# Block sums of the keys by one-column matmuls, transposes in two halves of 64 rows, and gate masks of 0 and 1

## The chip, the cores and the metric

The kernel runs on one core of a Trainium2 chip. The core has a matrix engine (TensorE, PE in the profile, with its weight loads listed apart as PEld), a vector engine (VectorE, DVE), an activation engine (ScalarE, ACT), a general engine (GpSimd, POOL), a sync engine that issues transfers (SyncE, SP), and 16 DMA engines. Tiles lie in SBUF; matmuls write to PSUM, which DVE and ACT read and POOL does not. Each engine works through its own list of instructions in order and waits on semaphores for the others. The metric is the device time of one execution in microseconds (us).

## The reference

Two layers follow each other. The first is block-sparse attention over 4 batches, 8 heads, 768 positions of width 64. Each query scores the means of the 12 key blocks of 64, keeps the three best blocks among its own and the earlier ones, adds its own block, and attends causally inside them. The second takes the real part of a two-dimensional Fourier transform of the attention's output, adds it to that output, normalises each row and runs a two-layer ReLU network of width 2048, with a residual.

```python
k_rep = k.reshape(B, H, n_blocks, block, D).mean(axis=3)
gate_scores = np.einsum('bhsd,bhnd->bhsn', q, k_rep)
gate_scores = np.where(causal, gate_scores, -1000000000.0)
top_idx = np.argsort(gate_scores, axis=-1)[..., -top_k:]
...
scores = np.where(mask, scale * np.matmul(q, k.transpose(0, 1, 3, 2)), -1000000000.0)
attn = np.exp(scores - np.max(scores, axis=-1, keepdims=True))
x = np.matmul(attn / (np.sum(attn, axis=-1, keepdims=True) + 1e-09), v)
...
u = x + np.real(np.fft.fft(np.fft.fft(x, axis=1), axis=2))
un = (u - mu) / np.sqrt(var + 1e-06)
return u + np.maximum(un @ w_ch1, 0.0) @ w_ch2
```

## The kernel before

The heads are taken in pairs: 16 pairs P of two heads e, four pairs to a batch b, pairs 0 to 3 being batch 0. A long string, `ORDER`, lists every step by hand as `name:arguments`, and the program walks it once and issues what each step holds; each engine's own order is what `ORDER` leaves of it. So where a step stands in `ORDER` decides what stands behind it on its engine.

The steps of one pair:

- `Lk`, `Lq`, `Lv`: SP issues the loads of keys, queries and values, three tiles deep for keys and queries, two for values.
- `tk`, `tq` (`a_tp`, L292): PE transposes the 128x128 fp32 pieces of keys and queries, six of each, into a PSUM tile `tp` of two banks. There are four such PSUM tiles for everything.
- `ks` (`a_sums`, L297): DVE sums the transposed keys over each block of 64, from PSUM, into `kr12`. `kh` (`a_half`) multiplies these 12 sums by a 0/1 tile and so lays them out by head.
- `kc` (L308, L311) copies the keys to fp16 on ACT, `qc` (L316) the queries to fp32 on DVE, `qs` on POOL to fp16.
- `g` (L335 for pairs 0 to 6, L342 later): the gate scores, fp32 matmuls on PE with 32 output rows each, one to each quarter of the array's columns. `gt` transposes them on DVE into `gt` and clears the blocks that lie in a query's future (a `min` with `lim` for pairs 0 to 6, three fills later). `gx` takes the eight largest of each row, `gl` compares with the third largest (`gl:P,0`) and multiplies with `oth` or `oth2`, which holds -60000 and, at the own block, 0 (`gl:P,1`); `gm` transposes back to `mt`.
- `s` (L409 and L421 for pairs 0 to 6; L414 later): scores. In pairs 0 to 6 the two heads' matmuls each use 64 rows of the array, upper half and lower half, into two banks; the mask is added by further 64-row matmuls of `mt` against `indz`. From pair 7 on the mask rows ride as rows 64 to 95 (`K`, on POOL) and each matmul has 96 rows.
- `e` (L431): the exponential on ACT. `d` (L437): the causal diagonal on POOL. `v` (L449): attention times values on PE. `x`: the division on DVE.

The steps of one batch: `fs`, `fd`, `f` fold the rows and columns on DVE; `y` (L519, L525) and `m` (L552, L553) are the two Fourier matmuls; `u` (L566) adds, `xu` (L578) scales to fp16 on ACT; then the rows are transposed, for batch 0 by PE (`xt`, `t_mm`, L585) with a DVE copy out (`un`, `t_copy`, L590), for the others by DMA. `w` (L629, L631) and `c` (L656) are the two network layers, 16 and 6 large steps per batch, `r` the ReLU, `o` the residual.

`w` of batch 0 is the first work that PE can do without waiting for each pair's chain; in `ORDER` of before it first stands behind the exponentials of pairs 0 to 5.

Of the kernel before, what the change touches and what calls it, by code (L numbers as in the profile page):

```python
# [15 lines left out]
NEG = -60000.0  # L16
# [12 lines left out]
def _consts_np():  # L29
# [22 lines left out]
    oth = np.where(np.arange(9)[:, None] + 3 != nn, NEG, 0.0)[None].repeat(128, 0)  # L52

    lim = np.where(nn[None, 4:8] > np.arange(3, 7)[:, None], -3e38, 3e38)
    lim = lim.reshape(1, 16).repeat(128, 0).astype(np.float32)

    indc = np.zeros((4, 32, 2, NB), np.float32)
    for g in range(4):
        for n in range(NB):
            indc[g, n, g % 2, n] = 1.0  # L60

    own = 2 * np.arange(5)[None, :] + 2 + (p // 64)[:, None]
    oth2 = np.zeros((128, 5, 2, 16), np.float32)
    oth2[:, :, :, 0:NB] = np.where(own[:, :, None, None] != nn, NEG, 0.0)
    ind = np.zeros((2, 32, S), np.float32)
    for e in range(2):
        ind[e, 16 * e:16 * e + NB] = nn[:, None] == (s[None, :] // 64)
    return dict(FS=fs.astype(np.float16), FD=fd.astype(np.float16),
                oth=oth.reshape(128, 108).astype(np.float16),
                lim=lim,  # L70
                indc=indc.reshape(128, 24).astype(np.float16),
                oth2=oth2.reshape(128, 160).astype(np.float16),
# [40 lines left out]
Lk:1 Lq:1 Lk:2 Lq:2 tk:0 ks:0 tq:0 Lq:3 Lk:3 kh:0 qc:0 iz:1 tk:1 qs:0 kc:0 g:0 ks:1 iz:0 gt:0 tq:1  # L113
kc:1 gx:0 Lq:4 Lv:0 Lk:4 Lv:1 kh:1 gl:0,0 tk:2 gl:0,1 gm:0 kc:2 qc:1 s:0,3 s:0,2 ks:2 e:0,3 qs:1
tq:2 Lq:5 Lk:5 s:0,5 qc:2 g:1 e:0,5 e:0,2 kh:2 s:0,4 gt:1 qs:2 s:0,0 e:0,4 gx:1 s:0,1 d:0,2 tq:3
gl:1,0 e:0,0 gl:1,1 tk:3 gm:1 e:0,1 d:0,0 qc:3 g:2 d:0,3 kc:3 d:0,5 s:1,5 gt:2 d:0,4 s:1,0 e:1,5
qs:3 ks:3 s:1,4 e:1,0 tq:4 d:0,1 gx:2 vc:0 e:1,4 s:1,3 qc:4 s:1,1 Lv:2 e:1,3 s:1,2 gl:2,0 kh:3
tk:4 gl:2,1 e:1,2 d:1,3 gm:2 g:3 d:1,4 ks:4 d:1,0 v:0 d:1,5 gt:3 vc:1 kc:4 gx:3 e:1,1 s:2,5 Lv:3
Lq:6 LF:0 Lq:7 Lk:6 Lk:7 LT:0 s:2,3 kh:4 gl:3,0 e:2,5 gl:3,1 s:2,4 e:2,3 d:1,1 x:0 tq:5 qs:4 e:2,4
g:4 d:2,3 gm:3 qc:5 s:2,0 d:2,4 s:2,2 d:1,2 e:2,0 gt:4 d:2,5 tk:5 vc:2 gx:4 e:2,2 s:2,1 ks:5 d:2,0  # L120
Lv:4 Lq:8 Lk:8 s:3,1 e:2,1 v:1 gl:4,0 kh:5 gl:4,1 kc:5 d:2,1 gm:4 d:2,2 s:3,2 x:1 e:3,1 vc:3 g:5
e:3,2 Lv:5 Lc:0 d:3,1 s:3,5 gt:5 s:3,0 fs:0,1 e:3,5 s:3,3 d:3,2 gx:5 e:3,0 s:3,4 fs:1,1 tq:6
gl:5,0 e:3,3 fs:0,0 v:2 gl:5,1 fs:1,0 e:3,4 d:3,3 qc:6 d:3,0 s:4,5 x:2 d:3,4 s:4,4 e:4,5 d:3,5
s:4,0 qs:5 v:3 e:4,0 gm:5 fs:2,0 fs:2,1 e:4,4 s:5,5 x:3 s:4,1 e:5,5 s:5,1 e:4,1 fd:2,0 s:4,2 s:5,0
fs:3,1 e:5,1 fs:3,0 s:5,2 fd:2,1 e:5,0 fd:3,1 s:4,3 fd:3,0 e:5,2 tk:6 f:0,1 f:0,2 e:4,3 Lk:9 Lq:9
tk:7 f:0,3 e:4,2 f:0,0 y:0,1 ks:7 pg:0 W:0 kc:6 y:0,0 tr:0,1 d:4,0 kc:7 d:4,4 d:4,5 ks:6 d:5,5
d:4,1 ty:0,1 tr:0,0 s:5,3 d:5,2 s:5,4 d:4,3 kh:6 W:1 ty:0,0 m:0,2 qs:6 e:5,3 u:0,2 m:0,1 vc:4
e:5,4 m:0,0 u:0,1 xu:0,2 d:5,4 tk:8 d:5,1 d:4,2 u:0,0 xu:0,1 d:5,0 xt:0,2 W:2 g:6 un:0,2 xu:0,0
xt:0,1 gt:6 tq:8 un:0,1 kc:8 xt:0,0 qc:8 tq:7 un:0,0 qs:8 v:4 Lq:10 Lk:10 Lv:6 Lq:11 qc:7 bn:0,3
w:0,4 d:5,3 qs:7 bn:0,1 w:0,5 r:0,4 gx:6 ks:8 w:0,6 r:0,5 gl:6,0 kh:7 gl:6,1 x:4 w:0,7 r:0,6 gm:6  # L130
w:0,3 r:0,7 s:6,5 r:0,3 s:6,1 e:6,5 s:6,3 e:6,1 kh:8 s:6,2 fs:4,0 bn:0,4 w:0,2 e:6,2 d:6,1 X:0
e:6,3 g:7 w:0,0 d:6,5 gt:7 r:0,2 d:6,3 vc:6 gx:7 s:6,4 r:0,0 vc:5 s:6,0 e:6,4 tk:9 Li:0 gl:7,0
Lv:7 tq:9 gl:7,1 e:6,0 gm:7 w:0,11 Lq:12 Lv:8 K:7 qc:9 kc:9 g:8 r:0,11 v:5 gt:8 d:6,0 ks:9 w:0,8
qs:9 gx:8 w:0,10 x:5 r:0,8 d:6,4 d:6,2 gl:8,0 s:7,5 s:7,2 r:0,10 kh:9 fs:4,1 w:0,1 bn:0,5 e:7,5
vc:7 e:7,2 tq:10 gl:8,1 Lv:9 r:0,1 X:1 gm:8 s:7,4 qc:10 w:0,15 d:7,2 e:7,4 K:8 bn:0,0 g:9 r:0,15
s:7,0 w:0,9 gt:9 e:7,0 gx:9 vc:8 tq:11 r:0,9 d:7,0 Lv:10 s:7,1 qc:11 d:7,5 tk:10 d:7,4 e:7,1
gl:9,0 s:7,3 ks:10 v:6 e:7,3 kh:10 gl:9,1 kc:10 gm:9 d:7,3 s:8,4 bn:0,2 d:7,1 w:0,12 vc:9 x:6
e:8,4 K:9 Lv:11 Lk:11 Lq:13 Lq:14 Lk:12 Lk:13 v:7 r:0,12 g:10 x:7 s:8,3 w:0,13 e:8,3 gt:10 nv:0
s:9,4 r:0,13 fs:5,1 s:9,1 fs:7,0 vc:11 w:0,14 e:9,4 fs:6,1 e:9,1 fs:7,1 s:8,1 fs:6,0 fs:5,0
c:0,2,0 r:0,14 fd:7,1 fd:6,1 e:8,1 gx:10 s:9,0 fd:7,0 s:9,2 e:9,0 fd:6,0 s:8,2 gl:10,0 c:0,3,0  # L140
f:1,3 e:9,2 f:1,2 e:8,2 gl:10,1 f:1,0 s:8,0 gm:10 s:9,3 d:8,2 e:8,0 y:1,1 d:8,1 d:9,0 e:9,3 nr:0
c:0,0,0 tr:1,1 ty:1,1 s:9,5 c:0,2,1 e:9,5 d:8,0 d:9,3 tk:11 K:10 s:8,5 c:0,1,0 Lk:14 ks:11 kc:11
# [32 lines left out]
r:3,8 w:3,13 r:3,1 r:3,4 w:3,6 w:3,10 w:3,9 r:3,10 r:3,13 w:3,5 r:3,6 w:3,14 r:3,5 w:3,12 c:3,2,0  # L175
r:3,12 r:3,9 r:3,14 c:3,0,0 w:3,15 c:3,4,0 r:3,15 c:3,1,0 c:3,0,1 c:3,1,1 c:3,5,0 o:3,0 od:3,0
o:3,1 c:3,3,0 od:3,1 o:3,5 od:3,5 c:3,4,1 c:3,2,1 o:3,4 od:3,4 c:3,3,1 c:3,5,1 o:3,3 od:3,3 o:3,2
od:3,2 o:3,6 od:3,6
"""
assert PT_W == 5376 and len(COL) == 42  # L180

# [606 lines left out]
```

## Time and profile before

| | |
|---|---|
| median of two timed runs | 297.85 us (297.19 and 298.51) |
| the profiled execution | 297.41 us, of which the span of its instructions 295.6 us |
| granted TensorE clock in the profile | 1.000 |

The span and the time differ by 1.8 us, which lie around the instructions. Read first the busy shares over the span in 40 slices (a slice is 7.4 us, a digit is tenths of it, 9 is 90% or more):

```profile
## 2 busy tenths in 40 slices
PE   8899999999999999999999999999999999999995
PEld 4566767765676556656757667446666554555453
DVE  2999999986988638987796577714493282700132
ACT  3698989749578841677788843165524250155000
POOL 2267528528776289064753363220303000110000
PEclk9999999999999999999999999999999999999999
DMA  8999999997999727477000005311000052300023
```

A busy PE is not PE at its peak, since matmuls overlap: a matmul of 512 columns takes 379 ns from start to end, but the next one may start after 216 ns. The costliest groups (line, engine, operation, tiles, shape, count, then busy us and mean ns of one, then the idle time before them):

```profile
L629 PE MATMUL h<-unT,w 128*128 128x512 f16 x256 | 85.1, 379 | 0.0
L656 PE MATMUL c<-w_sb,hT 128*128 128x512 f16 x368 | 83.8, 379 | 0.0
L431 ACT ACTIVATE pt<-sc 128x1024 f16<-128x1024 f32 (+1 forms) x96 | 83.3, 923 | 26.6 <-PE sc L414 19.7
```

### The profile page before, as it was taken

What the parts mean: (1) busy time and instruction counts of PE and PEld (TensorE: products, weight loads), DVE (VectorE), ACT (ScalarE), POOL (GpSimd) and SP (SyncE); (2) the same over time, 40 slices, a digit from 0 to 9 for tenths busy, and PEclk for the clock granted to TensorE, in tenths of its full rate; (3) what the DMA queues carried; (4) which work ended last, traced back from release to release, by engine and by line L of the source; (5) the groups of instructions that cost most, each with busy time, mean ns of one, the idle gap of its engine ahead of it and who ended that gap; (6) DMA issues with size and microseconds to landing.
All of it is one profiled execution on the core that took longest, in us unless ns stands there. A gap on an engine that the chain in (4) does not pass through costs nothing.

```text
span 295.6 us, 6738 instructions
## 1 busy us (share of the span) xinstructions
PE 286.5 (97%) x2633; PEld 180.2 (61%) x2633; DVE 192.5 (65%) x597; ACT 164.2 (56%) x205; POOL 111.1 (38%) x286
## 2 busy tenths in 40 slices
PE   8899999999999999999999999999999999999995
PEld 4566767765676556656757667446666554555453
DVE  2999999986988638987796577714493282700132
ACT  3698989749578841677788843165524250155000
POOL 2267528528776289064753363220303000110000
PEclk9999999999999999999999999999999999999999
DMA  8999999997999727477000005311000052300023
GB/s 197 268 228 230 262 245 199 195 230 118 226 185 211 168 55 186 118 164 176 3 0 2 0 9 136 38 72 71 2 1 2 32 103 44 142 0 2 0 91 125
DMA packets 93200, 33.53 MB, mean 113 GB/s; under 512 B 85936, under 2 KB 89968, under 8 KB 93168
## 3 DMA queue, kind: packets, MB, share of 16 engines
q1 hardware_dynamic: 87504, 28.47, 40.6%
q0 software_dynamic: 3664, 4.19, 9.1%
q10 hardware_dynamic: 2000, 0.44, 0.7%
q8 instruction: 21, 0.34, 0.5%
q14 instruction: 11, 0.09, 0.1%
HBM read 28.63 MB, written 6.29 MB: 118 GB/s over the span
## 4 chain that ended last, share of the span: by engine, by line
PE 84%; DVE 7%; ACT 6%; DMA 1%; issue 1%; DVEq 0%; ACTq 0%
PE c L656 26%; PE h L629 19%; PE h L631 10%; PE sc L414 7%; PE av L449 6%; ACT pt L431 5%; PE tp L292 5%; PE yp L519 2%; PE mx L552 2%; DVE q L316 2%; PE mx L553 1%; PE warmps L693 1%; DVE u L566 1%; PE g L342 1%; PE c L648 1%; PE sc L409 1%
## 5 line engine op out<-in xcount | busy, mean ns | idle before, releaser
L431 ACT ACTIVATE pt<-sc 128x1024 f16<-128x1024 f32 (+1 forms) x96 | 83.3, 923 | 26.6 <-PE sc L414 19.7
L629 PE MATMUL h<-unT,w 128*128 128x512 f16 x256 | 85.1, 379 | 0.0
L656 PE MATMUL c<-w_sb,hT 128*128 128x512 f16 x368 | 83.8, 379 | 0.0
L631 PE MATMUL h<-unT,w 128*128 128x256 f16 x256 | 69.7, 272 | 0.4 <-DMA unT<-x 0.4
L641 ACT ACTIVATE hT<-h 128x768 f16<-128x768 f32 x48 | 37.8, 813 | 43.7 <-PE h L631 43.7
L656 PEld LDWEIGHTS <-hT 128*128 128x128 f16 x368 | 35.6, 98 | 39.3 <-issue 0.5
L437 POOL TENSOR_SCALAR_AFFINE_SELECT pt<-pt 128x256 f16<-128x256 f16 x96 | 37.5, 414 | 58.5 <-ACT pt L431 57.6
L629 PEld LDWEIGHTS <-w 128*128 128x128 f16 x256 | 25.0, 97 | 29.2 <-issue 1.3
L668 DVE SCALAR_TENSOR_TENSOR u<-c,rs,u 128x512 f32<-128x512 f32 (+1 forms) x25 | 17.5, 725 | 31.2 <-PE c L656 30.4
L639 DVE TENSOR_SCALAR hT<-h 128x768 f16<-128x768 f32 x16 | 15.3, 955 | 29.7 <-PE h L631 29.6
L578 ACT ACTIVATE x<-u,nm 128x512 f16<-128x512 f32 x24 | 15.9, 715 | 22.5 <-DVE nm L572 22.3
L292 PE MATMUL tp<-id,nat 128*128 128x128 f32 x192 | 27.5, 284 | 0.6 <-ACT pt L431 0.3
L631 PEld LDWEIGHTS <-w 128*128 128x128 f16 x256 | 25.0, 98 | 4.3
L225 POOL TENSOR_SCALAR_AFFINE_SELECT qk<-mt 32x160 f16<-32x160 f16 x72 | 23.1, 341 | 10.8 <-DVE mt L386 9.1
L414 PE MATMUL sc<-qk 96*128 96x512 f16 (+3 forms) x144 | 26.8, 305 | 0.0
L225 POOL TENSOR_SCALAR_AFFINE_SELECT qk<-q 64x768 f16<-64x768 f32 (+1 forms) x25 | 20.6, 825 | 14.8 <-DVE q L316 14.1
L292 PEld LDWEIGHTS tp<-id,nat 128*128 128x128 f32 x192 | 22.2, 146 | 5.7 <-issue 1.6
L449 PE MATMUL av<-v,pt 128*128 128x65 f16 x672 | 23.0, 193 | 0.1
L449 PEld LDWEIGHTS <-pt 128*128 128x128 f16 x672 | 22.0, 97 | 1.7 <-POOL pt L437 0.5
L297 DVE TENSOR_REDUCE kr<-tp 128x12 f32<-128x768 f32 x16 | 15.1, 945 | 5.9 <-PE tp L292 5.9
L222 POOL TENSOR_TENSOR t<-vr,rs 128x6 f32<-128x6 f32 x12 | 2.4, 199 | 43.5 <-DVE rs L609 42.9
L414 PEld LDWEIGHTS <-qk 96*128 96x128 f16 x144 | 13.3, 97 | 8.9 <-issue 0.5
(95 smaller groups left out, 351.2 us busy)
## 6 DMA issues: line engine op xcount, KB each, us to landing
nat<-in_v_dram SPq DMA_DIRECT2D x16, 384.0 KB, 4.7
nat<-in_k_dram SPq DMA_DIRECT2D x31, 192.0 KB, 3.5
nat<-in_q_dram SPq DMA_DIRECT2D x31, 192.0 KB, 3.9
out_dram<-u SPq DMA_DIRECT2D x23, 256.0 KB, 2.1
w_sb<-in_moe_w_ch_dram POOLq DMA_DIRECT2D x2, 1024.0 KB, 10.2
w<-in_moe_w_ch_dram POOLq DMA_DIRECT2D x2, 768.0 KB, 8.4
fs_sb<-c_FS SPq DMA_DIRECT2D x1, 582.0 KB, 5.1
w<-in_moe_w_ch_dram POOLq DMA_DIRECT2D x1, 512.0 KB, 7.3
```

What stands on the lines that cost most here:

```text
L225: nc.gpsimd.affine_select(out=out, in_=in_, pattern=[[0, i] for i in n], base=0, channel_multiplier=0, compare_op=ALU.is_ge, fill=0.0)
L292: nc.tensor.transpose(ps[:, 128 * st:128 * st + 128], src[:, st, :], id32)
L414: nc.tensor.matmul(ps[:, e, co:co + q1 - q0], qk[0:96, e, 1, 128 * jt:128 * jt + 128], qk[0:96, e, 0, q0:q1], start=True, stop=True)
L431: nc.scalar.activation(out=d["pt"][:, o:o + 2 * n].rearrange("p (e c) -> p e c", e=2), in_=d["sc", i][:, :, 0:n], func=AF.Exp, scale=0.125)
L437: nc.gpsimd.affine_select(out=dg, in_=dg, pattern=[[0, 2], [1, 128]], base=0, channel_multiplier=-1, compare_op=ALU.is_ge, fill=0.0)
L449: nc.tensor.matmul(av[:, e, 66 * st:66 * st + 65], pt[:, co:co + 128], vv[:, e, jt, 0:65], start=(cnt == 0), stop=(cnt == 20))
L578: nc.scalar.activation(out=x_b[:, 2 * kp + k2, :], in_=u_b[:, k2, :], func=AF.Identity, scale=0.0625, bias=nm[:, k2:k2 + 1])
L629: nc.tensor.matmul(hp[:, 0:512], w1s, unT[:, dt, 0:512], start=(dt == 0), stop=(dt == NDT - 1))
L631: nc.tensor.matmul(hp[:, 512:768], w1s, unT[:, dt, 512:768], start=(dt == 0), stop=(dt == NDT - 1))
L641: nc.scalar.activation(out=hT, in_=hp, func=AF.Relu)
L656: nc.tensor.matmul(c_ps[b, g[0]][:, st - g[0], :], h_t[b, it][:, 128 * st:128 * (st + 1)], w2_sb[:, it, :], start=(it == 0), stop=(it == N ...
L668: nc.vector.scalar_tensor_tensor(out=o, in0=ps, scalar=st_t[b][1][:, st:st + 1], in1=o, op0=ALU.mult, op1=ALU.add)
```

## The change

1. `a_tp`: each 128x128 transpose becomes two of 64 rows, the upper into one bank of the PSUM tile and the lower into the other; everything that reads the tile does so through `tp_view`. For the keys of pairs 0 to 8 each of them is followed by matmuls of the same 64 rows against a column of ones: 12 fp32 matmuls of one output column per pair.
2. `a_sums` is left out for pairs 0 to 8; `a_half` reads the sums from PSUM.
3. The masks `lt` are 0 or 1; the -60000 has moved into the constants `indc` and `ind`. The own block is filled with 3e38 in `gt` after the maxima are taken and before the comparison, so the multiplication is gone, and with it `oth`, `oth2` and their loads. `lim` gives way to a strided fill.
4. `t_mm` is cut into 64-row transposes in the same way, and `t_copy` for batch 0 becomes two copies of half the size.
5. `ORDER` is rewritten down to the middle of the work on batch 1's second layer; its last 202 steps are the same. In the new one five of pair 6's six score tiles, the gate of pair 7 and `v:5` stand ahead of the first `w`, where before only pairs 0 to 5 and the steps up to `v:4` did; the first row statistics (`bn:0,3`) and the third load of `w_ch1`, which stood ahead of it, now stand behind.

```diff
-            indc[g, n, g % 2, n] = 1.0
+            indc[g, n, g % 2, n] = NEG
...
-        ind[e, 16 * e:16 * e + NB] = nn[:, None] == (s[None, :] // 64)
+        ind[e, 16 * e:16 * e + NB] = np.where(nn[:, None] == s[None, :] // 64, NEG, 0.0)
...
 def a_tp(P, who):
-    d["tp", who] = ps = pst([128, S], f"tp{who}_{P}")
+    d["tp", who] = ps = pst([128, 2, 512], f"tp{who}_{P}")
     for st in range(NST):
-        nc.tensor.transpose(ps[:, 128 * st:128 * st + 128], src[:, st, :], id32)
+        for h in range(2):
+            rows = slice(64 * h, 64 * h + 64)
+            nc.tensor.transpose(ps[:, h, 64 * st:64 * st + 64], src[rows, st, :], id32[rows, rows])
+        for h in range(2 if who == 1 and P < NSUM else 0):
+            rows = slice(64 * h, 64 * h + 64)
+            o = 64 * NST + st
+            nc.tensor.matmul(ps[:, h, o:o + 1], src[rows, st, :], ones[rows, :], start=True, stop=True)
+
+def tp_view(ps):
+    return ps[:, :, 0:64 * NST].rearrange("p h (st c) -> p st h c", c=64)
...
 def a_half(P):
+    if P < NSUM:
+        sums = pairs[P]["tp", 1][:, :, 64 * NST:64 * NST + NST].rearrange("p h (o st) -> p o st h", o=1)
+        tt((kr_s if P < NX else kr2_s)[P % NSLOT][:, :, 0:NB].rearrange("p e (st h) -> p e st h", h=2),
+           sums.to_broadcast([128, 2, NST, 2]), half.rearrange("p e (st h) -> p e st h", h=2), ALU.mult)
+        return
...
 def g_turn(P):
     if P < NX:
-        x = gt.rearrange("p (b n) -> p b n", n=32)[:, 0:4, 4:8]
-        tt(x, x, lim, ALU.min)
+        nc.vector.memset(gt[:, 4:136].rearrange("p (b c) -> p b c", c=33)[:, :, 0:4], -3e38)
...
 def g_less(P, j):
     if j == 0:
-        tt(l, gt, mx[:, :, 2:3].to_broadcast([128, 9 if P < NX else 10, NB]), ALU.is_lt)
-    else:
-        tt(l, l, o, ALU.mult)
+        if P < NX:
+            nc.vector.memset(gt[:, 3:300].rearrange("p (b c) -> p b c", c=33)[:, :, 0:1], 3e38)
+        else:
+            for h in range(2):
+                nc.vector.memset(gt[64 * h:64 * h + 64, 2 + h:172 + h]
+                                 .rearrange("p (b c) -> p b c", c=34)[:, :, 0:17:16], 3e38)
+        return
+    tt(l[:, :, 0:NB], gt[:, 0:nj * w].rearrange("p (j n) -> p j n", n=w)[:, :, 0:NB],
+       mx[:, :, 2:3].to_broadcast([128, nj, NB]), ALU.is_lt)
...
 def t_mm(b, kp):
-    for k2 in range(2):
-        for dt in range(NDT):
-            nc.tensor.transpose(ps[:, dt, 128 * k2:128 * k2 + 128],
-                                x_t[b][:, 2 * kp + k2, 128 * dt:128 * dt + 128], id16)
+    for dt in range(NDT):
+        for k2 in range(2):
+            for h in range(2):
+                rows = slice(64 * h, 64 * h + 64)
+                nc.tensor.transpose(ps[:, h, dt, 64 * k2:64 * k2 + 64],
+                                    x_t[b][rows, 2 * kp + k2, 128 * dt:128 * dt + 128],
+                                    id16[rows, rows])
 def t_copy(b, kp):
-        nc.vector.tensor_copy(out=un_t[b][:, :, 256 * kp:256 * kp + 256], in_=t_ps[b, kp])
+        dst = un_t[b][:, :, 256 * kp:256 * kp + 256].rearrange("p t (k h c) -> p t k h c", h=2, c=64)
+        for h in range(2):
+            nc.vector.tensor_copy(out=dst[:, :, :, h, :], in_=t_ps[b, kp][:, h, 0:NDT, :]
+                                  .rearrange("p t (k c) -> p t k c", c=64))
...
-    nc.scalar.dma_start(lim, dr["lim"].ap().rearrange("p (b n) -> p b n", n=4))
-    nc.scalar.dma_start(oth, dr["oth"].ap().rearrange("p (b n) -> p b n", n=NB))
...
-    nc.sync.dma_start(oth2, dr["oth2"].ap().rearrange("p (b e n) -> p b e n", e=2, n=16))
```

## The prediction

> **What bounds the kernel now.** I read the page first, then a table of stages for the part in which the other engines are full, then the groups of PE, then its order of time. The first line of the page says that PE is busy for 97% of the span:
>
> ```profile
> PE 286.5 (97%) x2633; PEld 180.2 (61%) x2633; DVE 192.5 (65%) x597; ACT 164.2 (56%) x205; POOL 111.1 (38%) x286
> ```
>
> In the order of time the first `w` starts at 58.6. The table of stages up to there (stage, its length, busy time of PE, PEld, DVE, ACT, POOL, the clock, the DMA share) shows another picture:
>
> ```profile
> 12.60:24.00 11.40, 10.92 (x154) 7.20 (x151) 10.96 (x38) 9.93 (x13) 7.19 (x15) 1.00 1.04 235
> 24.00:35.00 11.00, 10.48 (x199) 7.13 (x196) 10.35 (x50) 10.35 (x13) 7.12 (x14) 1.00 1.05 244
> 35.00:45.00 10.00, 9.24 (x182) 7.54 (x182) 9.26 (x25) 9.25 (x13) 2.32 (x5) 1.00 1.03 245
> 45.00:55.00 10.00, 9.16 (x102) 7.06 (x101) 9.62 (x24) 9.83 (x13) 8.25 (x17) 1.00 1.11 205
> ```
>
> DVE, ACT and the DMA engines are all nearly full. PE's busy time holds the latency of each matmul, so I count its own work by the spacing of matmuls: 512, 256 and 128 columns of fp16 take 379, 272 and 219 ns, so a column costs 0.42 ns, and the rest is latency that overlaps. For each kind of step ahead of the first `w` this gives, in us: `tk` 5.9, `tq` 5.9 (nine each, 0.66 a step), `g` 3.4, `s` 12.5 (the two heads side by side), `v` 6.2, `y` 2.5, `m` 2.6, `xt` 1.3, changes of array shape 3.2 (34, priced below): 43.5. With 3.9 of warm-up matmuls PE is idle for 11.2 of 58.6. The same count for all that follows gives 231.4 in the 237.0 that are left; 3.4 of the 5.6 over lie behind the last matmul. So the kernel is an early stage that ACT and DVE set, then PE without a gap.
>
> **What a 64-row step costs.** The rows that price it (the first four are groups: busy us and mean ns of one; the others stand in order of time: start and length of a run of equal instructions):
>
> ```profile
> L292 PE MATMUL tp<-id,nat 128*128 128x128 f32 x192 | 27.5, 284 | 0.6 <-ACT pt L431 0.3
> L292 PEld LDWEIGHTS tp<-id,nat 128*128 128x128 f32 x192 | 22.2, 146 | 5.7 <-issue 1.6 <-ACT pt L431 0.9 <-DVE q L316 0.6
> L335 PEld LDWEIGHTS g<-q,kr 128*32 128x32 f32 x56 | 1.1, 107 | 1.7 <-issue 1.1 <-DVE x L222 0.3 <-ACT pt L431 0.2
> L297 DVE TENSOR_REDUCE kr<-tp 128x12 f32<-128x768 f32 x16 | 15.1, 945 | 5.9 <-PE tp L292 5.9
> ...
> 13.94 0.20 PE L421 MATMUL sc<-mt,indz 64*128 64x32 f16 x4
> ...
> 14.70 0.10 PEld L409 LDWEIGHTS <-qk 64*128 64x128 f16 x2 [0.47 <-issue]
> 14.70 0.39 PE L409 MATMUL sc<-qk 64*128 64x512 f16 x2
> ...
> 64.99 0.27 PE L631 MATMUL h<-unT,w 128*128 128x256 f16 x1
> 65.20 0.23 PE L409 MATMUL sc<-qk 64*128 64x128 f16 x2
> ...
> 67.85 0.27 PE L631 MATMUL h<-unT,w 128*128 128x256 f16 x1
> 68.05 0.48 PE L342 MATMUL g<-q,krb 128*32 128x160 f32 x8
> ```
>
> At 14.70 two matmuls of 512 columns, of 0.38 each, end within 0.39, and two weight loads of 0.09 within 0.10: the upper and the lower 64 rows work at the same time, in both. At 65.20 and 68.05 a matmul starts 0.21 and 0.20 after one of 256 columns that occupies 0.11: a change of array shape costs 0.095, and PE does nothing in it.
>
> An fp32 transpose of 128 columns takes the next one 0.11 later, twice a column of fp16, so 64 columns take 0.055. Its weight load of 128 columns lasts 146 ns where 32 columns last 107: 0.4 ns a column, so 0.05 for the load itself. I take 0.057 for a half, whichever ends last. If halves overlap, six pairs of halves are 0.34 where six transposes are 0.66: 0.31 less. If they don't, 0.68. No row shows an fp32 pair of halves; the nearest are these fp16 pairs in the same two halves, and I take the overlap.
>
> A one-column sum has one column to stream, but its weights are the full 128. `g` has 56 records for 28 matmuls: fp32 goes in two passes, each with its load. So each of the six positions of `tk` takes three loads, 0.171 if halves overlap: 1.03, which is 0.37 more than now; 2.05 if they don't.
>
> The Trainium skill speaks against this in "TensorE: Matmul & The Clock Gate", section "LDWEIGHTS (loading the stationary operand)": a load takes the number of columns over 1.2, whatever the rows, so 107 ns for 128. The rows above contradict it, with 39 ns for 96 more columns. By the page a `tq` would stay at 0.64, `tk` would be 1.92, and the sum below 15 us worse. Its "TensorEngine Tiling (Array Packing)", section "Key Properties", says that changing the tiling mode drains the array; here that is the 0.095.
>
> **The sum on PE.** Ahead of the first `w`: `tk` 9.2, `tq` 3.1, `xt` 0.7 by the new price. The new order also brings forward one `g`, five `s` tiles and `v:5`: 0.3 + 1.7 + 1.2 = 3.2. Shape changes are 32, 3.0. That makes 46.4 against 43.5. Behind it: 3.2 less for what was brought forward; seven `tk` and seven `tq` at 0.31 less, 4.4; 38 shape changes for 22, because transposes now stand as islands of 64 rows among 128-row matmuls, +1.5. So 225.3 against 231.4, 6.1 less. The whole of PE's work falls by 3.2, from 275.0 to 271.8; the other 2.9 is idle time filled early.
>
> **When the first `w` starts.** DVE loses ahead of it eight sums of 0.945 (7.6), six multiplications by `oth` of 0.215 (1.3) and seven `lim` steps of 0.309, for fills like those of L356 to L358 at 0.065 each (about 0.9 for fourteen, so 1.3 net): 10.2. `a_half` now reads PSUM: 0.22 to 0.37 for 24 elements, taken as 0.30, nothing to count. The two half copies of `un` lie between 0.74 and 1.2 for 0.68, three times, at the end of the chain: +0.2 to +1.5, taken as 0.5. So DVE is no longer full. ACT is: between the first exponential and the last `xu` its list grows by one `kc` (two casts of 0.79) and two exponentials (1.03 and 0.39), 3.0 by durations and 2.7 as they overlap. Its idle time in the table is 1.5 + 0.7 + 0.8 + 0.2 = 3.2, of which the first 1.5 lies where `kc` waits for the DVE sum ("ACT qk L308 <- DVE kr L297" in the waits); that wait goes, and what is late next is ACT itself. So the last `xu`, which ends at 55.9, ends at 55.9 + 2.7 - 1.5 = 57.1, or between 55.4 and 58.6. Behind it stand the copy (0.7 and the 0.5) and on PE `s:6,3`, `s:6,2` and `v:5`, 2 us, largely beside it. I take the first `w` where it was, at 58.6, give or take 2.
>
> The removed loads of `lim`, `oth` and `oth2` (8, 27 and 40 KB) cost their issue on queues of ACT and SP; no wait in the profile ends on them, and the load that SP issues behind the last one, the keys of pair 9, is used 25 us after its issue. I count nothing; without that cover it would be 1.1, the time of the issue of `oth2`. The first `tk` runs at half the pace (0.21 from one transpose to the next at 5 us, later 0.11): it would take 2.0 for 1.3, and the first `kh` no longer waits for a sum of 0.9, so these cancel.
>
> Span: 295.6 - 6.1 = 289.5. With the 1.8 around it 291.3, against 297.41 of the same execution; the median stands 0.4 higher. I predict 291.5.
>
> **The rivals.**
>
> *ACT or the loads hold the first `w` back.* For: DMA is full to the first `w`, and the new list has more values (`Lv:6` and on) ahead of it. Up to `Lv:5` and with the first part of `w_ch1` it must move nine keys and queries of 0.39 MB each, six values of 0.39, 1.2 of constants and 1.05 of weights: 11.7 MB, at 228 GB/s 51 us; the second part and `Lv:6` make 13.7 and 60. Against: from pair 5 on, keys and queries had landed 3 us and more ahead of their use. Price: the first `w` at 62, 3.4 later: 295. Chance 0.17.
>
> *DVE and ACT both gain,* with the 3.2 of ACT's idle time gone and the list behind `w` better fed: `w` at 55.5, 288.5. Chance 0.14.
>
> *The fp32 halves don't overlap,* in loads or in matmuls: slower. Then `tk` is 2.05 nine times (+12.5), the other 23 steps gain nothing (+0.6), shape changes +1.3: 289 of PE work for 275. Ahead of `w` 58.6 of work; the early idle time can swallow some 7 of the 15 extra, so `w` starts near 66.5; 230 behind it and the 5.6: 302, so 304 as a time. The point from which it decides: with 7 us of idle time over the 54 positions of nine `tk`, PE sets the early stage once a position costs over 0.30. Chance 0.15.
>
> The change doesn't do what it says if the narrower transposes lose to shape changes: 14 steps at 0.31 against 0.19 each when they stand alone. This is in the forecast, and leaves 0.12 a step; its worst is 1.5 us of the 6.1.
>
> **How the numbers follow.** Forecast 0.54 (288.5 to 294.5); the rivals 0.17, 0.14 and 0.15. The range goes from 286.5 to 298: it leaves out most of the last rival and a twentieth below. About 2% can be told from no change, 291.9: the forecast lies on both sides of it, 0.29 and 0.25; with the better case faster is 0.43, with the late `w` and part of the last rival the same is 0.43, slower 0.14.
>
> **What would show it.** After: runs of six `tk` matmul pairs near 0.35 us and of `tk` with sums near 1.0; no 945 ns sum for pairs 0 to 8; the first `w` near 58.6 with pair 6's exponentials done; ACT over 95% from 13 to 57; PE without gaps behind. The prediction is wrong if weight loads of the two halves come 0.05 apart instead of together, if PE waits for a `nat` load, or if `w` starts past 61.

## The result, and the profile after

| | before | after |
|---|---|---|
| median of two timed runs | 297.85 us | 321.80 us (321.27 and 322.33) |
| profiled execution, its span | 297.41, 295.6 us | 321.27, 319.6 us |
| first exponential | 12.6 us | 17.8 us |
| first `y` | 45.0 us | 64.9 us |
| first `w` | 58.6 us | 86.3 us |
| first `w` to the end of the last matmul | 233.5 us | 228.8 us |

The changed kernel is slower: the ratio is 1.081, 95% interval 1.076 to 1.087, and the prediction's range of 286.5 to 298.0 does not hold it. The first `w` comes 27.7 us later; from there to the last matmul 4.7 us were gained, and what lies behind the last matmul is 1.0 longer. In some kernels below a few executions took over 1.5% longer than the fastest of the same kernel; the ratios given leave these out. Of the page after (busy times, then 40 slices of 8.0 us each):

```profile
span 319.6 us, 7594 instructions
...
PE 300.5 (94%) x3065; PEld 192.8 (60%) x3065; DVE 186.7 (58%) x592; ACT 165.0 (52%) x205; POOL 114.0 (36%) x286
...
PE   7999897497999999999999999999999999999994
...
DVE  1446768938487998598497347772456265700132
...
PEclk9569999669699999999999999999999999999999
DMA  9999599909869899775300000511100033300023
```

Look at the row PEclk, the granted clock: before it was 9 in every slice, now it is at 5 to 6 in slices 2 and 3, 8 and 9, and 11. PE's row has a hole (4) in slice 8, where DVE is at 9. The table of stages after (columns as before: PE, PEld, DVE, ACT, POOL, clock, DMA share, GB/s):

```profile
0.00:12.60 12.60, 10.18 (x101) 7.04 (x101) 2.52 (x13) 3.65 (x5) 2.50 (x18) 0.80 1.11 187
12.60:24.00 11.40, 11.20 (x158) 8.69 (x156) 6.10 (x32) 5.03 (x8) 2.43 (x4) 0.62 1.12 213
24.00:35.00 11.00, 10.09 (x208) 7.19 (x205) 7.48 (x34) 9.55 (x13) 6.07 (x13) 1.00 0.95 195
...
55.00:70.00 15.00, 9.92 (x104) 8.99 (x106) 10.07 (x28) 5.91 (x8) 6.07 (x14) 0.66 0.59 103
70.00:85.00 15.00, 11.99 (x218) 9.63 (x219) 10.55 (x30) 11.03 (x15) 5.87 (x10) 0.81 0.90 170
```

From 12.6 to 24 us DVE and ACT are idle for half of the time (10.96 and 9.93 of 11.4 before, now 6.10 and 5.03), PE is busy for 11.20 of 11.40, at a clock of 0.62. So this stage has changed its limit: PE sets it, and DVE's relief buys nothing. The groups of the new `tk` and `tq` (mean ns behind the busy time):

```profile
L281 PE MATMUL tp<-id,nat 64*128 64x64 f32 x384 | 29.4, 253 | 6.4 <-DVE gt L354 5.5
L281 PEld LDWEIGHTS tp<-id,nat 64*128 64x128 f32 x384 | 25.4, 179 | 12.1 <-DVE gt L354 5.9
...
L286 PE MATMUL tp<-ones,nat 64*128 64x1 f32 x216 | 20.3, 266 | 0.6 <-DVE ones L711 0.6
L286 PEld LDWEIGHTS tp<-ones,nat 64*128 64x128 f32 x216 | 20.3, 252 | 0.7 <-DVE ones L711 0.7
```

The sums (L286) are 216 records, 54 positions of four records each, and cover 20.3 us. (A position is what is done for one 128x128 piece: two half transposes and the sum matmuls of both halves.) One more thing in the trace is new: between 53 and 60 us one fold on DVE takes over nine times its length. The order of time there, DVE, POOL and PE (start, length, what):

```profile
52.91 6.72 DVE L211 TENSOR_TENSOR zw<-sd 128x768 f16<-128x768 f16 x3
59.56 0.47 DVE L354 STREAM_TRANSPOSE gt<-g 128x288 f32<-128x288 f32 x1
...
52.89 0.95 POOL L733 DMA_DIRECT2D w<-in_moe_w_ch_dram  x1
53.87 0.83 POOL L214 TENSOR_SCALAR_AFFINE_SELECT qk<-q 128x768 f16<-128x768 f32 x1
54.65 1.11 POOL L443 TENSOR_SCALAR_AFFINE_SELECT pt<-pt 128x256 f16<-128x256 f16 x3
...
60.08 0.90 PE L281 MATMUL tp<-id,nat 64*128 64x64 f32 x12 [5.47 <-DVE gt L354]
```

Three folds (`fd`) that take 0.55 each take 6.72 together; the second lasts from 53.38 to 58.54, 5.16 us. It starts inside `W:0`, the issue of the first network weights by POOL (52.89 to 53.84), and POOL works without a gap to 59.2. PE waits 5.47 us for `gt`, which stands behind the folds on DVE, and its clock is at half from 58.7 to 69.0. In all, 30.7 us ahead of the first `w` are at half clock.

### The profile page after: what moved, and what is told of

Its sections match the earlier page's. It is cut to its first block, busy times and chain, and to the rows that moved or that the text cites. A ratio compares the mean times of both kernels' runs of the same rounds, so it can differ in the third digit from the quotient of the medians.

```text
span 319.6 us, 7594 instructions
## 1 busy us (share of the span) xinstructions
PE 300.5 (94%) x3065; PEld 192.8 (60%) x3065; DVE 186.7 (58%) x592; ACT 165.0 (52%) x205; POOL 114.0 (36%) x286
## 4 chain that ended last, share of the span: by engine, by line
PE 87%; DVE 6%; ACT 3%; DMA 2%; issue 1%; SPq 0%
PE c L668 25%; PE h L641 17%; PE h L643 9%; PE av L455 7%; PE sc L420 7%; PE tp L281 5%; PE tp L286 3%; PE yp L525 3%; PE sc L415 2%; DVE zw L211 2%; DMA nat<-in_k_dram 2%; PE sc L427 2%; PE mx L558 1%; PE mx L559 1%; ACT pt L437 1%; DVE u L572 1%
## 5 line engine op out<-in xcount | busy, mean ns | idle before, releaser
L437 ACT ACTIVATE pt<-sc 128x1024 f16<-128x1024 f32 (+1 forms) x96 | 84.2, 919 | 48.2 <-PE sc L420 29.1
L443 POOL TENSOR_SCALAR_AFFINE_SELECT pt<-pt 128x256 f16<-128x256 f16 x96 | 38.4, 421 | 84.9 <-ACT pt L437 84.4
L281 PE MATMUL tp<-id,nat 64*128 64x64 f32 x384 | 29.4, 253 | 6.4 <-DVE gt L354 5.5
L281 PEld LDWEIGHTS tp<-id,nat 64*128 64x128 f32 x384 | 25.4, 179 | 12.1 <-DVE gt L354 5.9
L214 POOL TENSOR_SCALAR_AFFINE_SELECT qk<-mt 32x160 f16<-32x160 f16 x72 | 24.1, 356 | 11.2 <-DVE mt L392 7.6
L455 PE MATMUL av<-v,pt 128*128 128x65 f16 x672 | 23.9, 196 | 0.0
L286 PE MATMUL tp<-ones,nat 64*128 64x1 f32 x216 | 20.3, 266 | 0.6 <-DVE ones L711 0.6
L286 PEld LDWEIGHTS tp<-ones,nat 64*128 64x128 f32 x216 | 20.3, 252 | 0.7 <-DVE ones L711 0.7
L320 DVE COPY q<-tp 128x768 f32<-128x768 f32 x16 | 15.2, 949 | 8.9 <-PE tp L281 8.9
```

What stands on the lines that cost most here:

```text
L214: nc.gpsimd.affine_select(out=out, in_=in_, pattern=[[0, i] for i in n], base=0, channel_multiplier=0, compare_op=ALU.is_ge, fill=0.0)
L281: nc.tensor.transpose(ps[:, h, 64 * st:64 * st + 64], src[rows, st, :], id32[rows, rows])
L286: nc.tensor.matmul(ps[:, h, o:o + 1], src[rows, st, :], ones[rows, :], start=True, stop=True)
L437: nc.scalar.activation(out=d["pt"][:, o:o + 2 * n].rearrange("p (e c) -> p e c", e=2), in_=d["sc", i][:, :, 0:n], func=AF.Exp, scale=0.125)
L443: nc.gpsimd.affine_select(out=dg, in_=dg, pattern=[[0, 2], [1, 128]], base=0, channel_multiplier=-1, compare_op=ALU.is_ge, fill=0.0)
L455: nc.tensor.matmul(av[:, e, 66 * st:66 * st + 65], pt[:, co:co + 128], vv[:, e, jt, 0:65], start=(cnt == 0), stop=(cnt == 20))
```

## The experiments

Theory F: the sums take more of PE than predicted and let its clock fall. Rivals: the new order starves PE; the loads are slower. The first four runs undo the sums and the order, apart and together, and give the sums more to stream; each was timed once.

**Sums taken out, in the new order** (`NSUM = 0`, and `ks:P` put back just ahead of `kh:P` for pairs 0 to 8):

```diff
-    NSUM = 9
+    NSUM = 0
-... tk:0 Lk:3 tq:0 Lq:3 Lv:0 qc:0 iz:0 kh:0 tk:1 ...
+... tk:0 Lk:3 tq:0 Lq:3 Lv:0 qc:0 iz:0 ks:0 kh:0 tk:1 ...
```

> The changed kernel with the sums of all pairs on DVE again (NSUM = 0, each sum just ahead of its kh), so the one-column matmuls are gone; halves of 64 rows, masks and the new order stay. Theory A, the one-column matmuls slow the early stage (each position of tk 0.29 us with the full clock and 0.53 with half of it) and let the clock fall: the clock stays at 1.0 from 7 us on, the first w starts at 59 to 63 us, time 293 to 298. Theory B, the new order and the 5 us in which a DVE step waits at 53 us are to blame: the clock still falls, w stays past 75, time 308 or more.

309.27 us, first `w` at 74.3: theory B by the time. The sums are worth 12.5 of the loss in this order, and the other half stays; so does the half clock, 24 us of it ahead of the first `w`.

**The same with the order of before:**

> The changed kernel with the order of before and all sums on DVE: what is left of the change are the halves of 64 rows, the masks of 0 and 1 and the fills. By the prediction's price for halves (0.34 us for a tq) and a shape change (0.095) PE's work falls by 4 to 6 us and DVE's by 2.5 in the early stage: 291 to 295, clock at 1.0 throughout. Rival: the narrower transposes let the clock fall as well, or lose to shape changes: 298 or more.

307.22 us. First `w` at 60.8, nearly as in the kernel before, but 240.6 us behind it. On the chain that ended last stand waits for value loads of 5.7, 7.5 and 11.1 us. Halves and masks alone should not make loads slower; this was open. The clock is at half here too, from 7.7 to 17.9 us and from 99.9 to 103.3, with no sum on PE: halves alone can let it fall, as the rival expected.

**Sums by matmul in the order of before** (`a_sums` returns at once for pairs below 9):

> The changed kernel with the order of before; the sums of pairs 0 to 8 stay on PE. Theory A (one-column matmuls): the clock falls in the first 25 us as in the changed kernel, the first w past 70, time 308 to 322. Theory B (the new order): the clock holds or falls briefly, time 292 to 300.

311.82 us, first `w` at 72.3: 11.5 us later than without the sums. The clock is at half from 8.8 to 22.5 us, as theory A expected.

**Each sum matmul streams 96 columns of ones instead of one:**

```diff
-    ones = ctile([128, 1], FP, "ones")
+    ones = ctile([128, 96], FP, "ones")
-                nc.tensor.matmul(ps[:, h, o:o + 1], src[rows, st, :], ones[rows, :], ...)
+                nc.tensor.matmul(ps[:, h, o:o + 96], src[rows, st, :], ones[rows, :], ...)
```

> The changed kernel with each sum's matmul 96 columns wide in place of one (the moving operand is 96 columns of ones, each later matmul overwrites all but one column of the one before; the result is the same). Count of matmuls, loads and waits is unchanged; only the time that the array streams rises, from about 1 to 80 ns a pass, under a weight load of 85 to 95. If the clock falls because the one-column matmuls hardly stream, it now stays up in the first 25 us, a tk with sums takes 1.7 us and not 3.2, and the time falls to 300 to 312. If it falls for another reason (idle PE, the weight loads themselves) clock and time stay as they are, 320 to 325.

317.22 us. With 96 times as much to stream the kernel is faster: the half clock below 22 us is gone. The time is above the 300 to 312 expected: the fold still took 5.17 us, and the clock was at half behind it.

**The place of the loads.** In these traces the 256-byte packets of the loads took longer than before, from 4 us on, when PE has no work of the change yet. The change drops the tiles `oth`, `lim` and `oth2`, so the tiles allocated behind them move: the key tiles from byte 87552 of a partition, a multiple of 512, to 86976, which is 64 above a multiple of 128. Two runs tell it apart: the changed kernel with the old place, the kernel before with the new one (`gone` is the last constant ahead of the loads).

```diff
     gone = ctile([1, 4], F16, "gone")
+    ctile([128, 288], F16, "pad")     # pad_after; shift_before has 224
```

> The changed kernel with one unused tile of 576 bytes per partition behind the constants, so that the tiles of loaded keys start at byte 87552 again, a multiple of 512, as in the kernel before (the changed kernel has them at 86976, which is 448 above one). Theory A, where the loads land in SBUF sets their speed: the 256-byte packets of the loads, 18.0 ns each in the kernel before and 25 ns between 4 and 14 us in the changed one, are back at 18.0 ns; the first exponential moves from 17.8 to below 16.5 us, and the time from 321.8 to between 308 and 317 us. Rival B, the slower packets come from something else that the change did: packets stay at 24 to 26 ns and the time at 319 to 324 us.

> The kernel before with one unused tile of 448 bytes per partition behind the constants; nothing else differs, and the key tiles start 448 bytes above a multiple of 512, as in the changed kernel. Theory A (place in SBUF): 256-byte packets between 4 and 14 us rise from 18.0 to about 25 ns, and the time rises from 298 to between 301 and 310 us. Rival B (another cause): packets stay at 18.0 ns, the time within 1.5 us of 298.

The DMA view from 7 to 14 us, in the kernel before, in the changed one and in the shifted one (packets, bytes and mean rate; the main queue's packets and their time as a share of 16 engines):

```profile
DMA packets 7462, 1.87 MB, mean 267 GB/s; under 512 B 7462, under 2 KB 7462, under 8 KB 7462
...
q1 hardware_dynamic: 7453, 1.87, 118.2%
```

```profile
DMA packets 6024, 1.53 MB, mean 218 GB/s; under 512 B 6023, under 2 KB 6023, under 8 KB 6023
...
q1 hardware_dynamic: 6023, 1.51, 134.1%
```

```profile
DMA packets 6030, 1.50 MB, mean 215 GB/s; under 512 B 6030, under 2 KB 6030, under 8 KB 6030
...
q1 hardware_dynamic: 5886, 1.48, 129.0%
```

A share of 118.2% of 16 engines over 7 us, shared among 7453 packets, is 17.8 ns a packet; after it is 24.9, in the shifted kernel 24.5, in the padded one 17.8. That the place does it is shown in both directions. What it is worth was expected too high: it is small in these two kernels, `shift_before` 299.68 us, ratio 1.0048 (1.0018 to 1.0079); `pad_after` 320.43 us, 1.4 less than the changed kernel, which two runs of each hardly tell. The first exponential came at 16.8 there, 1.0 earlier.

Where the loads are awaited it is much. The order of before without sums, padded:

> The changed kernel's halves, masks and fills with the order of before and no sums by matmul (307.22 us as it was), with the unused tile of 576 bytes. Theory A (place in SBUF): packets at 18.0 ns, no waits on value loads of 5 to 11 us between 68 and 95 us, and 231.4 less some 6 us behind the first w: 291 to 297 us. Rival B: packets at 24 to 26 ns, 305 to 309 us.

298.31 us for 307.22 (one run); 0.5 more than before, no longer slower in a way that can be told (ratio 1.0014, 0.9983 to 1.0044), but not the 291 to 297 expected. The profiled execution kept the full clock; in eight of the ten the mean granted clock was 0.981 to 0.989, and seven of these eight took 297.8 to 299.2, so a half clock of that size is not what made 307.22.

**W:0 behind the folds.** In the order of before POOL issues the first weights behind `pg:0`, its wait for the folds; the new order puts it between them.

```diff
-... fs:3,1 fd:2,0 W:0 e:4,3 fd:3,0 ... tk:8 pg:0 e:5,5 ...
+... fs:3,1 fd:2,0 e:4,3 fd:3,0 ... tk:8 pg:0 W:0 e:5,5 ...
```

> The changed kernel with one step moved: W:0, by which POOL issues the load of the first network weights, stands behind pg:0, POOL's wait for the folds of batch 0, as it does in the kernel before, instead of ahead of it between the folds. Theory C, the fold of 5158 ns on DVE at 53.4 us is held up by POOL's work of that issue: no DVE operation above 1.5 us, the half clock of 58.7 to 69.0 us gone or shorter, the first w at 78 to 82 us instead of 86.3, and 313 to 318 us. Rival D, the late weights hold w: first w at 85 us or later, weights awaited, 320 to 326 us. Rival E, the long fold has another cause, such as POOL's causal diagonals: it stays at 5 us and the time at 320 to 323 us.

319.93 us. The long fold is gone (order of time on DVE):

```profile
54.63 2.53 DVE L210 TENSOR_TENSOR zw<-sd 128x768 f16<-128x768 f16 x3
57.08 0.47 DVE L353 STREAM_TRANSPOSE gt<-g 128x288 f32<-128x288 f32 x1
```

So the place of the issue made the long fold, as theory C had it. But the half clock of 58 to 68 us stayed, the first `w` came at 84.6, not at 78 to 82, and the time is above the 313 to 318 expected: that part of theory C was wrong. PE stood idle there for 1.27 us in place of 5.47, and the clock fell at 57.9, ahead of the next sums at 58.95.

**Parts put together.** From here on the 18 transfers that turn the rows of batches 1 to 3 are plain copies of the same bytes, so these batches go into the first layer unturned; all lie behind the first `w`. The control:

> A control for the runs beside it: the kernel before, with the 18 transposing transfers that turn the rows of batches 1 to 3 (un) replaced by plain copies of the same bytes, so that the rows of these batches go into the first layer unturned. All 18 lie behind the first w. Every theory: first w at 58.6 us as before, and the time within 2 us of 297.8; what it differs by is to be taken off the three other runs, which have the same replacement.

297.07 us, ratio 0.9986 (0.9971 to 1.0001): what the copies change is some 0.3 us, 0.9 at the edge of the interval. With it, in the old place of the loads:

> The changed kernel in its own order, without the sums by matmul (the DVE sums stand just ahead of each kh again), with the loads placed as in the kernel before, and plain copies in place of the turning of rows in batches 1 to 3. Against pad_old_order_no_sums (298.31 us, first w at 57.3 us) it has the new order. Theory F, the sums and the clock that they let fall are nearly the whole loss: 297 to 302 us, clock full after 20 us. Rival G, the new order by itself starves PE before the first w: 304 to 309 us, first w at 70 us or later, clock at half for more than 8 us.

307.00 us, first `w` at 71.5, half clock for 13.7 us: rival G by its numbers. But the run changes more than the order: the DVE sums stand directly ahead of their `kh`, where the order of before has three steps or more between them. From 12.6 to 55 us the chain of work that ended last runs for 25.4 us on DVE, 7.3 on PE and 2.6 on ACT; in `pad_old_order_no_sums` for 6.8 on DVE, 7.9 on DMA and 13.8 on ACT. So DVE sets this stage here, and no run has the new order with the DVE sums in another place.

> Halves, masks and the sums by matmul for the first nine pairs, in the order of before, with the loads placed as in the kernel before, and plain copies in place of the turning of rows in batches 1 to 3. Ahead of the first w it differs from pad_old_order_no_sums (first w at 57.3 us, 298.31 us) in the sums alone. Theory F: 54 positions at 0.23 us more than a plain pair of halves (0.285 against 0.06) are 12 us of PE work, and the clock falls to half below 20 us as in the changed kernel: first w at 66 to 72 us and 306 to 312 us. Rival G: 298 to 303 us, since PE had 11 us of idle time ahead of the first w that can take the sums in.

310.72 us, first `w` at 71.7: theory F, against 298.31 and 57.3 without the sums. From 12.6 to 55 us the chain that ended last now runs for 22.9 us on PE, where it was 8.6 in the kernel before: the sums have put PE on it.

> The changed kernel with three things mended at once: each sum matmul streams 96 columns of ones instead of one (317.22 us when alone), W:0 stands behind the folds (319.93 us alone), and the loads are placed as in the kernel before (320.43 us alone); with plain copies in place of the turning of rows in batches 1 to 3. If the three effects only add up, 4.6 + 1.9 + 1.4 less than 321.8: 313 to 315 us. If the half clock is what they share, no half clock is left ahead of the first w, which starts at 68 to 74 us: 303 to 309 us.

309.37 us, first `w` at 74.2, no half clock ahead of it. Singly the three were worth 4.6, 1.9 and 1.4, together 12.4: the half clock is what two of them share, since each alone leaves a stretch of it. PE waits as long behind the folds here as in `w0_behind_folds` (its row first), and keeps its clock:

```profile
57.61 0.73 PE L280 MATMUL tp<-id,nat 64*128 64x64 f32 x12 [1.27 <-DVE gt L353]
```

```profile
51.63 0.59 PE L281 MATMUL tp<-id,nat 64*128 64x64 f32 x12 [1.27 <-DVE gt L354]
```

So that wait need not halve the clock. But 309 is still 11.5 above before.

**What makes the sums and the order dear.**

> As plain_old_order_sums (310.72 us, first w at 71.7 us, half clock from 7.4 to 21.1 and 55.2 to 58.6), but each sum matmul streams 96 columns of ones instead of one. Theory H, the time that the sums take on PE at full clock is the larger part: no half clock, first w at 65 to 68 us, 303 to 307 us. Rival I, the half clock is nearly all of what the sums cost: first w at 58 to 62 us and 298 to 301 us.

306.59 us, first `w` at 66.7, clock 1.00 up to there: theory H. Of the 12.4 us that the sums cost in the old order 8.3 stay at full clock, some 1.3 of them because 96 columns make a `tk` 1.83 long for 1.68.

> As plain_no_sums (307.00 us, first w at 71.5 us), with W:0 behind pg:0 as in the kernel before. If the early issue of the weights is what the new order costs, the half clock of 50.4 to 57.3 us is gone, first w at 60 to 66 us and 298 to 302 us. If the order of the other steps is, 304 to 307 us.

306.10 us, first `w` at 71.7. Neither the issue nor the fold that it held is what the new order costs when DVE makes the sums.

> As plain_no_sums (307.00 us), but each half transpose of pairs 0 to 8 is issued twice in a row: some 6 us more work on PE ahead of the first w and the same values. Theory J, PE has so little to do in the new order that its clock falls, and that is what the order costs: no half clock from 9 to 17 us, half or less of the one at 50 to 57 us, and 300 to 306 us in spite of the added work. Rival K, the added work simply adds: 309 to 314 us.

311.19 us. The early half clock was gone; ahead of the first `w` 6.8 us of half clock were left of 13.7, and the time was 4.2 longer: rival K. So in this order without sums the clock is not the main cost: less half clock did not pay for some 6 us of added work. How much it costs is not shown.

**The other parts alone.**

> The kernel before with the masks of 0 and 1 and the fills alone: 128-row transposes, sums on DVE and the order of before; loads placed as before; with plain copies in place of the turning of rows in batches 1 to 3, so that it is compared with before_plain (297.07 us, first w at 58.7 us). DVE loses some 3 us ahead of the first w. If DVE sets the early stage beside ACT, first w at 56 to 57.5 us and 294 to 296 us; if ACT alone does, 296.5 to 298 us. Slower than 299 us would make the masks or fills part of the loss.

297.07 us, as much as `before_plain`; first `w` 0.9 earlier. The masks and fills cost nothing and give next to nothing.

> As pad_old_order_no_sums (298.31 us: order of before, halves, masks and fills, no sums by matmul), with the tile gt widened by 64 bytes, so that the value tiles too start at a multiple of 128 (113408; there 113344, 64 above one; 113280 in the kernel before), and with plain copies in place of the turning of rows in batches 1 to 3. There PE stood idle for 4.4 us behind the first w, of which 2.6 in one wait on POOL, which had waited 5.0 us on value loads. Theory A (place in SBUF, for values too): POOL's waits on values fall below 2.5 us, PE's idle time behind the first w below 1.5 us, and 293.5 to 296 us, faster than before_plain (297.07). Rival L, the value loads are late because of their order in the queue: 297 to 299 us.

297.97 us (295.36 to 303.30), ratio 0.9956 (0.9930 to 0.9982). The eight shorter executions have a median of 296.8, between the two ranges, so the time does not decide. In the profiled execution, one of the longer ones (301.12), POOL still waited 4.7 us on values and PE 2.3 on POOL, and packets from 76 to 90 us took 19.7 ns for 20.2 without the widening: this speaks for rival L.

> As plain_masks_only (297.07 us), with the tile gt widened by 64 bytes, so that the value tiles too start at a multiple of 128. PE had next to no idle time behind the first w there, so all theories: 296 to 297.5 us.

296.75 us, ratio 0.9962 (0.9946 to 0.9978): as expected. So in the order of before the halves gain nothing over 128-row transposes (0.9956 and 0.9962), and no kernel here is more than 0.5% under the one before. In ten of the twelve executions with halves the granted clock was 0.982 to 0.991, with 128-row transposes always 0.997 or more.

**The account.** Each kernel's stretch up to its first `w` as one row of the table of stages; `pad_old_order_no_sums`, then with sums of 96 columns, then of one column, then the mended new order, then the changed kernel:

```profile
0.00:57.30 57.30, 47.09 (x881) 33.32 (x881) 49.25 (x174) 47.11 (x59) 29.07 (x71) 1.00 1.05 227
```

```profile
0.00:66.70 66.70, 58.98 (x1098) 46.10 (x1099) 43.20 (x166) 47.98 (x59) 29.26 (x71) 1.00 0.96 205
```

```profile
0.00:71.70 71.70, 64.06 (x1098) 50.54 (x1099) 43.12 (x166) 48.18 (x59) 29.16 (x71) 0.88 0.90 194
```

```profile
0.00:74.20 74.20, 62.52 (x1184) 48.76 (x1185) 49.85 (x184) 52.05 (x64) 35.83 (x77) 1.00 0.93 203
```

```profile
0.00:86.30 86.30, 72.50 (x1184) 57.09 (x1185) 51.95 (x184) 52.10 (x64) 34.70 (x79) 0.82 0.92 177
```

Behind the stretch stand its length and PE's busy time in it. The same row of the kernel before has 53.30 in 58.60. Put side by side with the time from the first `w` to the end of the last matmul (clock: of the profiled execution, ahead of the first `w`; time: the median):

| kernel | PE busy ahead | idle | clock | behind | time |
|---|---|---|---|---|---|
| before | 53.3 | 5.3 | 1.00 | 233.5 | 297.85 |
| halves and masks, old order | 47.1 | 10.2 | 1.00 | 236.7 | 298.31 |
| with sums of 96 columns | 59.0 | 7.7 | 1.00 | 233.2 | 306.59 |
| with sums of one column | 64.1 | 7.6 | 0.88 | 233.2 | 310.72 |
| new order, `W:0` behind, 96 columns | 62.5 | 11.7 | 1.00 | 228.9 | 309.37 |
| new order, one column (`pad_after`) | 71.3 | 13.1 | 0.84 | 228.9 | 320.43 |
| the changed kernel | 72.5 | 13.8 | 0.82 | 228.8 | 321.80 |

From top to bottom: halves and masks 0.5, the sums' work at full clock 8.3, the half clock that comes with one column 4.1, the new order with `W:0` in its early place 9.7 (310.72 to 320.43), the place of the loads 1.4. With the clock full and `W:0` behind, the order costs 2.8 (306.59 to 309.37); the other 6.9 of its 9.7 are half clock and the held fold, which no run here parts further. Rows with two timed runs may be off by 1 us (those of `pad_after` lie 2.0 apart).

## Why the prediction was wrong

**Right: the overlap of the halves and their price.** The two halves of a transpose start mostly 3 to 6 ns apart, in loads and in matmuls. A step behind the first `w`, in the kernel before and in `plain_old_order_wide`, each with the step that follows it:

```profile
105.86 0.82 PE L292 MATMUL tp<-id,nat 128*128 128x128 f32 x6
106.51 0.28 PE L414 MATMUL sc<-qk 96*128 96x128 f16 x2
```

```profile
88.59 0.58 PE L281 MATMUL tp<-id,nat 64*128 64x64 f32 x12
89.11 0.61 PE L422 MATMUL sc<-qk 96*128 96x512 f16 x2
```

From start to next step this is 0.52 for 0.65: 0.13 saved with the changes of array shape in it, where the prediction left 0.12. In the early stage, at full clock, the twelve starts of a `tq` lie within 0.31 to 0.37 us; with a last step of 0.06 this is 0.37 to 0.43 for 0.71 before (six starts within 0.60 and 0.11): 0.28 to 0.34 saved, where the prediction had 0.31. DVE's busy time fell from 192.5 to 186.7, with 4.6 of the held fold in it.

**Near by luck: the part behind `w`.** The 4.7 us gained there look like the 6.1 forecast. But in the order of before halves and masks bring this part from 233.5 to 233.2 only, where the prediction had 2.9 for the halves (4.4 less 1.5). The new order brings it to 228.9, 4.3 for the 3.2 written, and what it brings forward must be done earlier.

**The step that failed first: the price of a sum position, 0.171.** Here the sums at full clock, in the old order:

```profile
35.80 0.22 PE L281 MATMUL tp<-id,nat 64*128 64x64 f32 x2
35.85 0.34 PE L286 MATMUL tp<-ones,nat 64*128 64x1 f32 x4
36.05 0.25 PE L281 MATMUL tp<-id,nat 64*128 64x64 f32 x2
36.14 0.34 PE L286 MATMUL tp<-ones,nat 64*128 64x1 f32 x4
36.34 0.25 PE L281 MATMUL tp<-id,nat 64*128 64x64 f32 x2
```

From one position to the next it is 0.285; the six run from 35.80 to the next step at 37.48, 1.68 us where the prediction had 1.03 and 0.71 was spent before. Nine `tk` are 5.9 us dearer than written. The first pass starts 0.09 behind the transposes, the second 0.085 later, the next transposes 0.11 later: each of the three steps of a position takes about 0.1. What they stream is not it: 96 columns for one make a position 0.305 instead of 0.285. The prediction had taken 0.057 for each step, the price of a half transpose, from the lengths of two loads (146 less 107 ns for 96 columns). For a half transpose that was near, 0.062 to 0.07 from one to the next in a `tq`; for the two passes of an fp32 sum, with loads of the same 64x128 shape, it was not. Why a pass holds the next one longer than a transpose does no run shows. The rule of the Trainium skill that it set aside ("TensorE: Matmul & The Clock Gate", section "LDWEIGHTS (loading the stationary operand)": columns over 1.2, 107 ns) gives, by estimate, 0.32 a position and 1.92 a `tk`, nearer to 1.68 than 1.03; for a `tq` it gives 0.64 where 0.43 was measured at most, and there the rows were nearer. With the page's figure the prediction's own sum would have been an estimated 306.5, with the right sign.

The rival that ended slower priced a `tk` at 2.05 through halves that don't overlap. That mechanism is false. Its point of decision, 0.30 a position, counted on PE's idle time to take in what costs less. A position is 0.285 at full clock, just under it, and 0.53 at half. Yet the sums cost 8.3 us at full clock: PE took in 11.9 us more of busy time ahead of the first `w` (47.1 to 59.0), and its idle time fell by 2.5 only (10.2 to 7.7). The idle time lay where the sums could not use it.

**The step that was missing: the clock.** Every price was taken at the 1.00 of before. In the changed kernel it is at half from 7.5 to 21.2 us, and there a `tk` takes 3.0 to 3.2 us. These two rows, at 61.60 in the changed kernel, show a position at half clock:

```profile
61.60 0.35 PE L281 MATMUL tp<-id,nat 64*128 64x64 f32 x2
61.74 0.53 PE L286 MATMUL tp<-ones,nat 64*128 64x1 f32 x4
```

"The first `tk` runs at half the pace ... so these cancel" was the place where it could have been seen: the first exponential came at 17.8, not at 12.6. That the sums of one column keep the clock down is shown by `wide_sums` and `plain_old_order_wide`, where 96 columns keep it up in the early stage. They are not the only thing that does: without any sums on PE the halves had 3.4 us of half clock, from 9.7 to 13.1, in the profile of `aligned_halves`, and 10.2 us in `old_order_no_sums`. The Trainium skill's same page, section "Part 1: The HAM clock gate", says that a monitor of PE's activity halves the clock after an idle window of 3.4 us. The stretches here are 3.4, 6.8, 10.2 and 13.7 us long, multiples of it. But this is the stage from 10 to 20 us in `plain_old_order_sums`:

```profile
10.00:20.00 10.00, 9.53 (x114) 7.32 (x113) 4.06 (x18) 3.92 (x5) 1.22 (x2) 0.50 1.06 239
```

PE is busy by its records for 9.5 of 10 us at a clock of 0.50, so a busy record does not by itself keep the clock up. What does is not shown.

**"The removed loads cost nothing".** True of their issue. But their tiles went too, and the place of all later tiles with them: 1.4 us here, 0.5% in the kernel before, and 8.9 us, by a single run, in the kernel whose loads are awaited.

**What was not looked at: a step that is moved.** `W:0` was moved ahead of `pg:0`, the wait that keeps its issue off the folds. The prediction counted the order's effect on PE's and ACT's lists and not on POOL's. The first `w` "where it was, at 58.6, give or take 2" fell with these four and with the new order itself, which costs 2.8 us even with the clock full and `W:0` behind; why is open. That ACT would be late next was wrong too: it was idle for half of the second stage.

## What to carry to other kernels

A matmul of one column is not free: here a position with sums of one column took only 7% less than one with 96. Price it by the start-to-start distance of matmuls of the same kind, and where no row has that kind, leave a wide range. Idle time of PE, added up over a stage, does not say that work moved there finds a place in it: look for the waits that it could fill. Very short matmuls can also take PE's clock away, and then the matmuls around them are dearer too: read the granted clock of the changed kernel first. And an edit that drops a constant or reorders issues moves addresses and DMA issues too: look at where load tiles land, and at what stands between a wait and the issue that it guarded.

## What the runs showed of the hardware

- A 256-byte packet into a tile at a multiple of 512 takes 17.8 ns, into one 64 above a multiple of 128 24.5 to 24.9. The Trainium skill, "DMA: Bandwidth & Descriptors", section "How a descriptor splits into AXI transactions", splits a transfer into transactions of 256 bytes that start at multiples of 256. It says this of what is read; here it is the place written that counts, and a packet into a tile 192 above a multiple of 256, as the keys' tiles of after lie, would need two. But the value tiles of before lie 128 above a multiple of 256, and from 76 to 90 us, when they are loaded, the main queue's packets still took 18 ns (58.5% of 16 engines over 14 us for 7188 packets); in `shift_before`, where they lie 64 above a multiple of 128, 22.7.
- One DVE operation with two inputs in SBUF was held for 5.16 us, through eight operations of POOL, when it started during POOL's issue of a weight load; without that issue the same operations took turns, 0.75 on DVE and 0.72 on POOL. The Trainium skill, "SBUF — State Buffer", section "SBUF: two separate sides", says that such a DVE operation and GpSimd share a port under a lock that one instruction holds. The waiting agrees; that it lasted over eight instructions in a row is more than that rule tells, and why is open.
- PE's clock fell under fp32 matmuls of one column although PE's records left hardly a gap (9.5 of 10 us busy, clock 0.50), and did not under the same loads with 96 columns (9.2 of 10 us, clock 1.00). With 64-row transposes and no such sums the mean granted clock was 0.981 to 0.989 in eight of ten executions, with 128-row ones 0.997 or more in all of twelve.
